# Seven products instead of eight for chunks 8 to 11, with a planner on new costs

## The chip, the cores and the metric

One core of one Trainium2 chip runs the kernel. The metric is the device time of one execution in microseconds. Four runs of the kernel before gave 288.5 to 291.41 us, median 289.25.

## The reference

Two stages follow each other. The first is a linear attention with decay (batch 4, 8 heads, 768 steps, head width 48); the second is a mixture of 4 experts on the 3072 x 384 result.

```python
for t in range(S):                       # attention
    cur = einsum('bhd,bhe->bhde', u * kt, vt)
    y[:, :, t] = einsum('bhd,bhde->bhe', rt, state + cur)
    state = w[None, :, :, None] * state + einsum('bhd,bhe->bhde', kt, vt)
x = y.transpose(0, 2, 1, 3).reshape(B * S, H * D)
p = domain_probs / (domain_probs.sum(-1, keepdims=True) + 1e-09)
for e in range(E):                       # experts; w1 384 x 1024, w2 1024 x 384
    h = maximum(x @ w1[e], 0.0)
    out += p[:, e:e + 1] * (h @ w2[e])
```

## The kernel before, in words

**Tiling.** Time is cut into 24 chunks of 128 steps: chunk `ci` belongs to batch `ci % 4` and is the `ci // 4`-th of it. Four chunks, one per batch, make a group of 512 rows (`sc`, 0 to 5) for the experts.

**Attention of a chunk** (lines 361 to 653). R, K and V are loaded by SyncE (L229). VectorE scales R and K by powers of w ("scale", L394 for chunks from 8 on). GpSimd multiplies R, K and u (L406, L414), VectorE sums over the head ("dcoef", L427), and GpSimd multiplies V by it ("dv", L432). R and K are transposed by TensorE for the first chunks and by a DMA from chunk 8 on (L439). TensorE makes the scores (L506), from chunk 8 on for two chunks in one go; VectorE masks them (L523 for the even chunk, 1024 wide; L520 for the odd one, two halves of 512). TensorE makes Y from the state and the scores (L546, L553), VectorE adds dv (L568), and the state is brought up to date by TensorE (L626), VectorE (L635) and GpSimd (L645).

**Experts.** For groups 0 and 1 (`sc < SCALED`), Y is transposed as it is; the first layer is L700 or L706, its relu is ScalarE's (L715, L717), the second layer is L737, and p enters as its result leaves PSUM (L746, L748). From group 2 on, Y is first multiplied by p of each expert ("Xs", four per chunk, L588 on ScalarE or L590 on VectorE), and a DMA transposes each half (L598, "Xout"), so that the second layer may sum over experts in PSUM. Each half has one buffer (`Yse0`, `Yse1`): the next chunk's Xs waits for the transpose of this one.

**Second layer from group 2 on.** For `sc < FIRST` (only group 2) it is direct: per chunk and expert 8 matmuls of 384 columns (L967, "l2s"), and one ScalarE copy per chunk (L974). For the later groups it is a 2 x 2 block scheme with seven products (`products`, L844 on): the four blocks are two chunks by the even and odd halves of the hidden width, and w2 is cut in the same way and into column halves of 192. VectorE makes sums of hidden blocks ("sum", L873, four per pair of chunks, in halves of the experts for the first pair), and once for all, eight sums of w2's blocks ("mix", L817). TensorE makes the products (L904, 16 matmuls of 192 columns each, in two jobs of 8). Results go through chains in one PSUM bank (`ONTO`), with copies by ScalarE (L925) and adds by VectorE (L927) in between. The last mix overwrites a block of w2, and so waits until all direct second layers are through.

**What sets the order.** Every engine's order is fixed at build time by a list-scheduling planner (L991 on). Each piece of work is a job with a cost per engine, needs, buffers taken and dropped, and a rank, the lower the earlier. The planner keeps a clock per engine, starts the job of lowest rank that is ready and fits, and multiplies costs by `SLOWER` after its own time 85, but for sums, Xs and mixes. `GATES` holds back the scaling of a pair of chunks from 8 on until a named piece of expert work is done. A job with costs for several engines goes to the one that takes it first. On the chip each engine then follows its list in order, and waits only for data and buffers.

**PSUM.** `mm` has four banks, shared by first-layer groups, products and second layers; `tr` one; `ys` one, for Y and state products; `At` two, for the even chunk's scores. The odd chunk's scores take one bank of `tr` and one of `mm`.

Of the kernel before, what the change touches and what calls it, by code (L numbers as in the profile page):

```python
# [19 lines left out]
def kernel(  # L20
# [14 lines left out]
    B, H, S, D = r.shape  # L35
    HD = H * D
    C = 128
# [73 lines left out]
    mask = consts.tile([128, 128], BF16)  # L111
# [10 lines left out]
    for b in range(B):  # L122
# [13 lines left out]

    GATES = [3, 4, 9, 4, 5, 6, 6, 24]
    WARM, NSPIN = 6.6, 6  # L140
    TAIL = {"T": 0.27, "V": 0.17, "A": 0.20, "P": 0.17, "S": 0.0}
    DMAT = 8
# [3 lines left out]
    ATT = ("scale", "ruk_a", "ruk_b", "dcoef", "dv", "T", "Tout", "At", "mask", "Y", "Yout", "X",  # L146
           "Xout", "Sm", "Sv", "S")
    SLOTS = [(0, 0, 1), (1, 0, 0), (0, 1, 1), (1, 1, 1), (2, 0, 0), (2, 1, 0), (3, 0, 0), (3, 1, 0)]
    FIRST = 3
    SCALED = 2  # L150
    ONTO = {6: 1, 5: 6, 3: 5, 4: 7}
    MIX_RANK = 18.0
    XS_ON = {'A': 0.61, 'V': 0.51}
    MIX_ON = {'V': 1.4}
    SCALE_US = 1.2
    VB_ON = {'A': 0.42, 'P': 0.5}
    XS_RANK = 0
    SUM_RANK = -60
    NSH = 4
    SEQ_S = (((1, 0), (3, 0), (2, 0), (1, 1), (3, 1), (2, 1), (4, 0), (4, 1)),  # L160
             ((1, 2), (3, 2), (2, 2), (4, 2)))
    LATE, SLOWER = 85.0, {"V": 1.13, "P": 1.06, "A": 1.15}
    SLOTS += [(e, sc, 0) for sc in range(2, SCALED) for e in range(E)]
    ORDER_P = (1, 2, 6, 7, 4, 5, 3)
    SEQ_P = ((0, 1, 0), (0, 2, 0), (0, 7, 0), (0, 1, 1), (0, 2, 1), (0, 7, 1), (0, 6, 0), (0, 6, 1), (0, 4, 0),
# [5 lines left out]
                 mm=4, xTe=3, hTs=3, oacc=6, Yse0=1, Yse1=1, Tn=2)  # L171
# [7 lines left out]
    def job(name, on, run, needs=(), rank=0.0, takes=(), drops=(), moves=None,  # L179
            behind=()):  # L180
        j = Job()
        j.behind = behind
        j.name, j.on, j.run, j.needs, j.rank = name, on, run, list(needs), rank
        j.takes, j.drops, j.moves = takes, drops, moves
        for k in drops:
            tokens[k] = tokens.get(k, 0) + 1
        j.pad = 0.0
        ci = name[1] if isinstance(name, tuple) and name[0] in ATT else -1
        if ci >= SUB:

            j.pad = PAD_PE if "T" in on else PAD
        j.no = len(jobs)
        assert name not in jobs
        jobs[name] = j
# [37 lines left out]
    at_of = {}  # L232
# [128 lines left out]
    def attention(ci):  # L361
# [4 lines left out]
        rk = float(ci)  # L366
# [25 lines left out]
        us = 0.48 if ci < SUB else 0.65  # L392
# [96 lines left out]


        paired = ci >= DMAT
        tags = ("tr", "mm") if paired and ci % 2 else ("At", "At")

        def at():

            for x in (ci - 1, ci) if paired else (ci,):
                for j in range(2):
                    if paired and x == ci:
                        tag = ("tr", "mm")[j]
                        tl["At", x, j] = psum.tile([128, NP, C], F32, tag=tag, bufs=slots[tag], name="At_ps")  # L500
                    else:
                        at_free.remove(j)
                        tl["At", x, j] = At_all[:, j]
                for q in range(NP):
                    for j in range(2):
                        nc.tensor.matmul(tl["At", x, j][:, q, :],  # L506
                                         tl["RKT", x][j * P2:(j + 1) * P2, 1, q, :],
                                         tl["RKT", x][j * P2:(j + 1) * P2, 0, q, :],
                                         start=True, stop=True)

        split = not paired or ci % 2
# [15 lines left out]
        last = ci + 1 if paired and ci % 2 == 0 else ci  # L527
        if paired and ci % 2:
            job(("At", ci), {"T": 0.64}, at, [("T", ci - 1, 1), ready], on_pe,
                (("At", ci - 1, 0), ("At", ci - 1, 1), ("tr", ci, 0), ("mm", ci, 1)),  # L530
                (("RKT", ci - 1), ("RKT", ci)))
        elif not paired:
            job(("At", ci), {"T": 0.42}, at, [ready] + ([("Tout", ci, 0)] if ci < SUB else []), on_pe,
                (("At", ci, 0), ("At", ci, 1)), (("RKT", ci),))
        for j in range(2 if split else 1):
            job(("mask", ci, j), {"V": 0.61 if split else 1.18}, mk(j), [("At", last)],
                rk - 0.5, (("AtM", ci),) if j == 0 else (), ((tags[j], ci, j),) if split else (("At", ci, 0), ("At", ci, 1)),
                behind=(("mask", ci, 0),) if j else ())

# [34 lines left out]
        sc = ci // SUB  # L574
# [28 lines left out]
        else:  # L603
            tag = "mm" if ci < SUB else "tr"
# [45 lines left out]
        if c == 0:  # L650
            job(("S", ci), {"V": 0.56}, sv, [("Sm", ci), ("Yout", SUB - 1)], rk + 2, (), (("ys", "S", ci),))
        else:
            job(("Sv", ci), {"V": 0.56}, sv, [("Sm", ci)], rk - 0.1, (("Tn", ci),), (("ys", "S", ci),))
            job(("S", ci), {"P": 1.1}, sp, [("Sv", ci)], rk - 0.5, (), (("Tn", ci),))

    y_sb = weights.tile([128, 3 * HD], BF16)
    y_free, y_at = [0, 1, 2], {}
# [186 lines left out]
    def products(sc, q, at0):  # L844
# [12 lines left out]
        at_of = {m: of[m, 0] for m in ORDER_P}  # L857
        no = s_no[0] % (NSH // 2) * 2
        s_no[0] += 1
        s_tok = [(f"S{no + hf}", sc, q) for hf in range(2)]  # L860
# [5 lines left out]
        def sum_job(k, hf):  # L866
            hs = (0, 1) if hf == 2 else (hf,)

            def run():
                o, x, y, op = {1: (None, A21, A22, ALU.subtract), 3: (A21, A21, A11, ALU.subtract),  # L870
                               2: (A11, None, A11, ALU.subtract), 4: (A12, A12, A11, ALU.add)}[k]
                o, x, y = (s1_of(hf) if z is None else a_of(z, hf) for z in (o, x, y))
                nc.vector.tensor_tensor(o, x, y, op=op)  # L873
            needs = all_cast + [n for h in hs for n in relus[h]]
            if k == 3 and q:
                needs.append(("C", sc, 0, 5))
            if k in (2, 4):
                needs += [("P", sc, q, 1 if k == 2 else 2, h) for h in hs]
            job(("sum", sc, q, k, hf), {"V": 1.26 if hf == 2 else 0.74}, run, needs,
                at_of[{1: 6, 3: 6, 2: 6, 4: 3}[k]] + SUM_RANK, tuple(s_tok[h] for h in hs) if k == 1 else (),  # L880
                tuple(x for h in hs for x in hts[h]) + (tuple(s_tok[h] for h in hs) if k in (1, 2) else ()),
                behind=(s_last[0],) if s_last[0] else ())
            s_last[0] = ("sum", sc, q, k, hf)
            for h in hs:
                sum_at[k, h] = s_last[0]
# [30 lines left out]
        for m in ORDER_P:  # L916
            at = at_of[m]

            def c_job(m, s, h, first, drop=()):
                def run():  # L920
                    oacc(c1)
                    o = tl["oacc", c1 // 2][:, s, h * DH:(h + 1) * DH]
                    ps = tl["P", sc, q, m]
                    if first:
                        nc.scalar.copy(o, ps)  # L925
                    else:
                        nc.vector.tensor_add(o, o, ps)  # L927
                needs = [("P", sc, q, m, 1)] + ([] if first else [("C", sc, q, {2: 1, 5: 7, 4: 6}[m])])
                job(("C", sc, q, m), {"A": 0.35} if first else {"V": 0.36}, run, needs, at - 90,
                    (("oacc", c1 // 2),) if m == 1 else (), tuple(("mm", "P", sc, q, x) for x in drop))  # L930
            if m == 1:
                c_job(1, 0, 0, True)
            elif m == 2:
                c_job(2, 0, 0, False, (2,))
                if c2 == TOTC - 1:
                    store(c1, [("C", sc, q, 2)], 0, DH)
            elif m == 6:
                c_job(6, 1, 0, True)
            elif m == 7:
                c_job(7, 1, 1, True)  # L940
            elif m == 5:
                c_job(5, 1, 1, False)
            elif m == 4:
                c_job(4, 1, 0, False, (7,))
                store(c2, [("C", sc, q, 4), ("C", sc, q, 5)])
            else:
                c_job(3, 0, 1, True, (1,))
                if c2 == TOTC - 1:
                    store(c1, [("C", sc, q, 3)], DH, Dm)
                else:  # L950
                    store(c1, [("C", sc, q, 3), ("C", sc, q, 2)])
# [26 lines left out]
    for sc in range(SCALED, NSC):  # L978
        at = 8 * (sc - SCALED) + len(SLOTS)
# [19 lines left out]
    avail = {"T": 3.7, "V": 4.5, "A": 3.3, "P": 1.5, "S": 0.6}  # L999
# [41 lines left out]
    now, seq, n_done = 0.0, 1, 0  # L1041
# [7 lines left out]
    def start(e):  # L1049
# [3 lines left out]
        while waiting[e]:  # L1053
            it = heapq.heappop(waiting[e])
            j = it[2]
# [10 lines left out]
        if got is not None and now < HURRY:  # L1066

            us = got.on[e]
# [8 lines left out]
        j = got  # L1077
# [3 lines left out]
                held.add(t)  # L1081
                free[t[0]] -= 1
        us = j.on[e] * (2.0 if e == "T" and now < WARM and j.name not in ("wmm", "umm") else 1.0)
        if e in SLOWER and now > LATE and j.name[0] not in ("sum", "Xs", "mix"):
            us *= SLOWER[e]
        if j.moves:
            taken, end = dma(now, us, *j.moves)
            us = taken - now + 0.04
# [90 lines left out]
```

## Time and profile before

| | |
|---|---|
| profiled execution | 289.8 us, span 287.8 us |
| TensorE busy | 279.9 us |
| VectorE busy | 181.3 us |
| ScalarE busy | 168.2 us |
| GpSimd busy | 105.5 us |
| first-layer matmuls L706 (512 columns) | 484 records, 113.7 us busy |
| direct second layer of group 2, L967 | 128, 21.9 us busy |
| seven products, L904 (three groups) | 672, 62.7 us busy |
| Xs on VectorE, L590 | 36, 21.1 us busy |
| Xs on ScalarE, L588 | 28, 16.7 us busy |
| operand sums, L873 | 36, 31.4 us busy |
| weight mixes, L817 | 8, 7.5 us busy |

Busy time of a group is counted from the records: neighbours of one engine overlap a little, so sums of busy time run above the stretch that the group fills. Weight loads have a row of their own (PEld) and overlap the matmuls (PE). The chain of waits goes back from the last instruction to what released it each time, and lists the pieces in order of time. "DVE a <- DMA b: total, times, longest" in the list of waits means that VectorE sat idle before a until b's transfer was there. Times in the stretches and the timeline count from the start of the span.

### The profile page before, as it was taken

What the parts mean: (1) busy time and instruction counts of PE and PEld (TensorE: products, weight loads), DVE (VectorE), ACT (ScalarE), POOL (GpSimd) and SP (SyncE); (2) the same over time, 40 slices, a digit from 0 to 9 for tenths busy, and PEclk for the clock granted to TensorE, in tenths of its full rate; (3) what the DMA queues carried; (4) which work ended last, traced back from release to release, by engine and by line L of the source; (5) the groups of instructions that cost most, each with busy time, mean ns of one, the idle gap of its engine ahead of it and who ended that gap; (6) DMA issues with size and microseconds to landing.
All of it is one profiled execution on the core that took longest, in us unless ns stands there. A gap on an engine that the chain in (4) does not pass through costs nothing.

```text
span 287.8 us, 6434 instructions
## 1 busy us (share of the span) xinstructions
PE 279.9 (97%) x2558; PEld 187.6 (65%) x2578; DVE 181.3 (63%) x305; ACT 168.2 (58%) x300; POOL 105.5 (37%) x127
## 2 busy tenths in 40 slices
PE   8898999999999999999999999999999999999995
PEld 3776655866775556444666554699745799544995
DVE  4976967667859978858544897788417473010760
ACT  4672968576848444788641489714588611799210
POOL 2884244462996745046563469801000000000000
PEclk9999999999999999999999999999999999999999
DMA  7998999999999576998859995902530401100011
GB/s 151 238 292 248 320 287 256 217 275 248 232 168 223 110 176 145 214 214 113 162 90 211 210 194 104 154 6 83 139 73 17 95 2 56 57 0 0 2 70 41
DMA packets 130145, 42.41 MB, mean 147 GB/s; under 512 B 118186, under 2 KB 130092, under 8 KB 130116
## 3 DMA queue, kind: packets, MB, share of 16 engines
q1 hardware_dynamic: 130100, 42.01, 66.1%
q8 instruction: 20, 0.33, 0.5%
q14 instruction: 9, 0.07, 0.1%
q10 hardware_dynamic: 16, 0.00, 0.0%
HBM read 26.79 MB, written 4.72 MB: 110 GB/s over the span
## 4 chain that ended last, share of the span: by engine, by line
PE 87%; SPq 6%; DMA 3%; DVE 2%; issue 1%; POOL 0%; ACT 0%; DVEq 0%; ACTq 0%
PE hT_ps L706 36%; PE M_ps L904 19%; PE out_ps L737 14%; PE out_ps L967 7%; PE hT_ps L700 4%; SPq L229 4%; DMA stg<-in_moe_w_dram 3%; PE At_all L506 1%; PE Y_ps L553 1%; PE St_ps L626 1%; SPq L246 1%; PE Y_ps L546 1%; SPq L243 1%; DVE stg L590 1%; PE RKT_ps L458 1%
## 5 line engine op out<-in xcount | busy, mean ns | idle before, releaser
L717 ACT ACTIVATE hAll<-hT_ps 128x512 bf16<-128x512 f32 x168 | 98.6, 597 | 24.8 <-PE hT_ps L706 19.3
L706 PE MATMUL hT_ps<-stg,w_sb 128*128 128x512 bf16 x372 | 85.3, 379 | 0.7
L706 PEld LDWEIGHTS <-w_sb 128*128 128x128 bf16 x504 | 47.4, 98 | 52.2
L904 PEld LDWEIGHTS <-hAll 128*128 128x128 bf16 x576 | 47.6, 98 | 0.8
L737 PE MATMUL out_ps<-w_sb,hAll 128*128 128x384 bf16 x256 | 45.7, 326 | 1.0 <-POOL w_sb L82 1.0
L406 POOL TENSOR_TENSOR ruk<-RKin 128x384 f32<-128x384 f32 x24 | 26.2, 1094 | 46.5 <-DMA RKin<-in_k_dram 27.6
L737 PEld LDWEIGHTS <-hAll 128*128 128x128 bf16 x256 | 24.1, 98 | 16.0 <-issue 1.1
L925 ACT COPY o_sb<-M_ps 128x192 f32<-128x192 f32 x24 | 7.6, 318 | 42.1 <-PE M_ps L904 42.1
L432 POOL TENSOR_TENSOR dv<-Vt,dcoef 128x384 f32<-128x384 f32 x24 | 20.6, 861 | 25.5 <-ACT stg L588 19.7
L706 PE MATMUL hT_ps<-xTe,w_sb 128*128 128x512 bf16 x112 | 28.4, 379 | 0.4
L645 POOL TENSOR_TENSOR S<-Tn,wC 64x192 bf16<-64x192 f32 x32 | 23.2, 725 | 9.5 <-DVE Tn L635 8.3
L904 PE MATMUL M_ps<-w_sb,hAll 128*128 128x192 bf16 x288 | 26.5, 246 | 0.0
L590 DVE TENSOR_SCALAR stg<-dv,p_nat 128x384 bf16<-128x384 f32 x36 | 21.1, 616 | 6.4 <-DMA stg<-stg 6.2
L414 POOL TENSOR_TENSOR ruk<-ruk,U_sd 128x384 f32<-128x384 f32 x23 | 24.3, 1061 | 1.0
L748 DVE SCALAR_TENSOR_TENSOR o_sb<-out_ps,p_nat,o_sb 128x384 f32<-128x384 f32 x24 | 14.6, 614 | 11.7 <-PE out_ps L737 11.7
L967 PE MATMUL out_ps<-w_sb,hAll 128*128 128x384 bf16 x128 | 21.9, 326 | 0.0
L588 ACT ACTIVATE stg<-dv,p_nat 128x384 bf16<-128x384 f32 x28 | 16.7, 610 | 6.9 <-DMA stg<-stg 6.0
L700 PE MATMUL hT_ps<-xTe,w_sb 128*128 128x128 bf16 x288 | 18.0, 219 | 0.2
L715 ACT ACTIVATE hAll<-hT_ps 128x512 bf16<-128x512 f32 x24 | 14.2, 597 | 6.0 <-PE hT_ps L700 5.1
L700 PEld LDWEIGHTS <-w_sb 128*128 128x128 bf16 x288 | 16.7, 98 | 1.1 <-ACT w_sb L78 0.3
L967 PEld LDWEIGHTS <-hAll 128*128 128x128 bf16 x128 | 12.1, 98 | 7.7
L394 DVE TENSOR_TENSOR RK_sb<-RKin,W_both 128x768 bf16<-128x768 f32 x16 | 16.7, 1061 | 0.1
(90 smaller groups left out, 324.6 us busy)
## 6 DMA issues: line engine op xcount, KB each, us to landing
stg<-in_moe_w_dram SPq DMA_DIRECT2D x16, 576.0 KB, 5.9
RKin<-in_k_dram SPq DMA_DIRECT2D x24, 192.0 KB, 3.8
Vt<-in_v_dram SPq DMA_DIRECT2D x24, 192.0 KB, 3.9
RKin<-in_r_dram SPq DMA_DIRECT2D x24, 192.0 KB, 4.2
out_dram<-o_sb SPq DMA_DIRECT2D x23, 192.0 KB, 2.0
stg<-in_moe_w_dram SPq DMA_DIRECT2D x8, 384.0 KB, 6.1
stg<-stg SPq DMA_TRANSPOSE x32, 2.8
RKT<-RK_sb SPq DMA_TRANSPOSE x16, 3.3
```

Of the source, the lines that this page charges most:

```text
L394: job(("scale", ci, 0), {"V": SCALE_US}, lambda: nc.vector.tensor_mul(RK[:, :, :, 0:D], tl["in", ci], W_both), [("Rt", ci), ("Kt", ci), (" ...
L406: nc.gpsimd.tensor_mul(tl["ruk", ci], tl["Rt", ci], tl["Kt", ci])
L414: nc.gpsimd.tensor_mul(tl["ruk", ci], tl["ruk", ci], U_sd)
L432: nc.gpsimd.tensor_mul(tl["dv", ci], tl["Vt", ci], tl["dcoef", ci].to_broadcast((128, H, D)))
L590: nc.vector.tensor_scalar(o, tl["Ysb", ci], scalar1=p_nat[:, e, n_p:n_p + 1], scalar2=None, op0=ALU.mult)
L645: nc.gpsimd.tensor_mul(S_new[pr, :, cl], Tn2[pr, tn_at[ci], :, cl], wC[pr, :, None].to_broadcast((P2, NP, D)))
L700: nc.tensor.matmul(ps[:, i, :], w1_sb[:, e, db, (fb + i) * 128:(fb + i + 1) * 128], xTe[:, db, s0, :], start=(i == 0 and db == 0), stop=(i ...
L706: nc.tensor.matmul(ps[:, 0:n, :].rearrange("p a b -> p (a b)"), w1_sb[:, e, db, fb * 128:(fb + 1) * 128], xTe[:, x0 + db, s0:s0 + n, :].re ...
L717: nc.scalar.activation(hTs[:, fb, s0:s0 + n, :], ps[:, 0:n, :], AF.Relu)
L737: nc.tensor.matmul(ps, relu_tile(e, sc)[:, fb, s, :], w2_sb[:, e, fb, :], start=(fb == 0), stop=(fb == NFB - 1))
L904: nc.tensor.matmul(tl["P", sc, q, m], st, moving(m, hf, n), start=(hf == 0 and n == 0 and m not in ONTO), stop=(hf == 1 and n == 7), skip_ ...
L967: nc.tensor.matmul(tl["o", ci], relu_tile(e, sc)[:, fb, s, :], w2_sb[:, e, fb, :], start=(e == 0 and fb == 0), stop=(e == E - 1 and fb == ...
```

## The change

It moves group 2 (chunks 8 to 11) from the direct second layer to seven products (`FIRST` 3 to 2), so that no direct one of the later kind is left, puts all Xs on ScalarE, changes costs in the planner, lengthens there VectorE's sums, scalings, mixes and Xs by up to 0.6 of what GpSimd is still busy, exchanges the two banks of the odd chunk's scores, and gives the first two operand sums of each group a rank of 0.0 above their place instead of -60, so that they no longer go ahead of masks.

```diff
-    GATES = [3, 4, 9, 4, 5, 6, 6, 24]
+    GATES = [3, 5, 8, 8, 16, 17, 7, 23]
...
-    FIRST = 3
+    FIRST = 2
...
-    MIX_RANK = 18.0
-    XS_ON = {'A': 0.61, 'V': 0.51}
-    MIX_ON = {'V': 1.4}
-    SCALE_US = 1.2
+    MIX_RANK = 16.0
+    XS_ON = {'A': 0.61}
+    MIX_ON = {'V': 0.97}
+    SCALE_US = 0.97
...
+    EARLY_SUM = 0.0
...
+    SHARED = 0.6
...
-        tags = ("tr", "mm") if paired and ci % 2 else ("At", "At")
+        tags = ("mm", "tr") if paired and ci % 2 else ("At", "At")
...
-                        tag = ("tr", "mm")[j]
+                        tag = ("mm", "tr")[j]
...
-                (("At", ci - 1, 0), ("At", ci - 1, 1), ("tr", ci, 0), ("mm", ci, 1)),
+                (("At", ci - 1, 0), ("At", ci - 1, 1), ("mm", ci, 0), ("tr", ci, 1)),
...
-            job(("mask", ci, j), {"V": 0.61 if split else 1.18}, mk(j), [("At", last)],
+            job(("mask", ci, j), {"V": 0.61 if split else 1.09}, mk(j), [("At", last)],
...
-            job(("Sv", ci), {"V": 0.56}, sv, [("Sm", ci)], rk - 0.1, (("Tn", ci),), (("ys", "S", ci),))
-            job(("S", ci), {"P": 1.1}, sp, [("Sv", ci)], rk - 0.5, (), (("Tn", ci),))
+            job(("Sv", ci), {"V": 0.5}, sv, [("Sm", ci)], rk - 0.1, (("Tn", ci),), (("ys", "S", ci),))
+            job(("S", ci), {"P": 1.3}, sp, [("Sv", ci)], rk - 0.5, (), (("Tn", ci),))
...
-            job(("sum", sc, q, k, hf), {"V": 1.26 if hf == 2 else 0.74}, run, needs,
-                at_of[{1: 6, 3: 6, 2: 6, 4: 3}[k]] + SUM_RANK, tuple(s_tok[h] for h in hs) if k == 1 else (),
+            job(("sum", sc, q, k, hf), {"V": 1.23 if hf == 2 else 0.7}, run, needs,
+                at_of[{1: 6, 3: 6, 2: 6, 4: 3}[k]] + (EARLY_SUM if k in (1, 3) and not q and not hf else SUM_RANK), tuple(s_tok[h] for h in hs) if k == 1 else (),
...
-                job(("C", sc, q, m), {"A": 0.35} if first else {"V": 0.36}, run, needs, at - 90,
+                job(("C", sc, q, m), {"A": 0.3} if first else {"V": 0.33}, run, needs, at - 90,
...
-        if e in SLOWER and now > LATE and j.name[0] not in ("sum", "Xs", "mix"):
+        if e in SLOWER and now > LATE and j.name[0] not in ("sum", "Xs", "mix", "scale"):
             us *= SLOWER[e]
+        if e == "V" and now > LATE and j.name[0] in ("sum", "scale", "mix", "Xs"):
+            us += SHARED * min(us, max(0.0, avail["P"] - now))
```

## Prediction

> **What bounds the kernel now.** I read the page first, then the chain that ended last, then the busy time in stretches of 8 us, then the waits.
>
> From the page, engine totals and two of the forty-slice rows:
>
> ```profile
> PE 279.9 (97%) x2558; PEld 187.6 (65%) x2578; DVE 181.3 (63%) x305; ACT 168.2 (58%) x300; POOL 105.5 (37%) x127
> ...
> PE   8898999999999999999999999999999999999995
> ...
> PEclk9999999999999999999999999999999999999999
> ```
>
> TensorE is busy 279.9 of 287.8 us, in nine tenths or more of every slice after the first ones, at its full clock. Busy is not proof of peak, so I check the pace: in the chain, the 512-wide first-layer products stand as 12 in 2.59 us, 0.216 us each, and no other engine but TensorE sits on the chain for more than a few us after 32 us. A stall put in is therefore paid in full, and TensorE work taken out is gained in full, as long as nothing new is late.
>
> From the chain, in order of time (start, length, what, count): the direct second layer of chunks 8 to 11 (L967), and two blocks of seven-product work (L904), of chunks 16 to 19 and 20 to 23:
>
> ```profile
> 138.71 1.30 PE out_ps L967 x8
> ...
> 140.38 2.60 PE out_ps L967 x16
> ...
> 143.15 2.60 PE out_ps L967 x16
> ...
> 145.92 2.60 PE out_ps L967 x16
> ...
> 148.69 2.60 PE out_ps L967 x16
> ...
> 151.46 6.50 PE out_ps L967 x40
> ...
> 158.52 2.71 PE out_ps L967 x16
> ...
> 226.99 18.48 PE M_ps L904 x224
> ...
> 266.19 18.49 PE M_ps L904 x224
> ```
>
> The same work for four chunks is 128 instructions in 1.30+2.60x4+6.50+2.71 = 20.91 us one way, and 224 in 18.48 the other.
>
> **The change part by part.**
>
> *FIRST 3 to 2: chunks 8 to 11 get seven products.* It removes 16 jobs of 8 matmuls (128 x 384 columns, 20.91 us) and 4 ScalarE copies, and adds 28 jobs of 8 (224 x 192 columns), 12 VectorE sums, 6 VectorE adds and 8 ScalarE copies. On TensorE: 18.48 - 20.91 = **-2.4 us**. A rule speaks against it. The Trainium skill, "TensorE: Matmul & The Clock Gate", section LDWEIGHTS, gives a weight load as columns/1.2 ns: 107 ns for 128 columns, and its section on the back-to-back issue gap says that load and product together set the spacing. If each of 224 products took its load's 107 ns, they would cost 23.9 us, and the change would lose 3.0. The rows decide: the loads do show 98 ns each, but 8 us of the seven-product stretch hold 100 products:
>
> ```profile
> 232.00:240.00 8.00, 8.00 (x100) 8.00 (x98) 5.04 (x7) 0.96 (x3) 0.00 (x0) 1.00 0.14 52
> ```
>
> That is (columns: stretch, its length, then busy of PE, PEld, DVE, ACT, POOL) 80 to 82.5 ns per product with PEld also full, so loads overlap each other; 18.48 is measured twice and I take it.
>
> *The eight weight mixes (L817) and sums need VectorE earlier.* The mixes were spread over 116 to 162 us, two of them held until L967 was through; now all eight, four 768-wide scalings, the masks and two sums stand before the first product. Tally for the first layer of chunks 8 to 11 up to the last mask that TensorE needs there: 1 eviction 0.61, 8 mixes x 0.95, 4 scalings x 0.95, 2 wide masks x 1.22, 4 narrow x 0.68, 2 half sums x 0.69, 2 dcoef x 0.54, 2 Y adds x 0.55 = 20.0, less about 0.08 for each of 24 neighbours that overlap (two mixes stand as 1.81) = 18. TensorE in the same stretch: 32 groups x 0.648, two pairs of score products x 0.55, three Y x 0.37 = 22.9. About 5 us of room, part of which goes into waiting for inputs. The layout of the queues leaves the closest Y job some 1 us behind its mask. Cost: 0; without the cover, about 1 us.
>
> *VectorE beside GpSimd.* The Trainium skill, "GPSIMD Engine Reference", section Specifications, says that GpSimd shares VectorE's SBUF interfaces and contends with instructions that have two SBUF inputs, and sums, mixes and scalings are such. The trace has both prices for a half sum, GpSimd busy and idle:
>
> ```profile
> 175.57 0.88 DVE L873 TENSOR_TENSOR hAll<-hAll 128x1024 bf16<-128x1024 bf16 x1
> ...
> 187.18 0.69 DVE L873 TENSOR_TENSOR hAll<-hAll 128x1024 bf16<-128x1024 bf16 x1
> ```
>
> The new sums are 16 halves' worth, so 0 to 3.2 us more of VectorE. GpSimd is busy 60% where they now stand, so some 1.9:
>
> ```profile
> 136.00:144.00 8.00, 8.00 (x70) 4.85 (x69) 4.37 (x9) 5.09 (x10) 3.83 (x5) 1.00 0.80 154
> 144.00:152.00 8.00, 8.00 (x60) 5.03 (x59) 3.75 (x6) 4.01 (x8) 4.98 (x7) 1.00 0.62 105
> ```
>
> VectorE under the new products: 16 x 0.61 + 1.9 + 6 adds x 0.28 + 4 state adds x 0.5 + two small ones 1.0 = 16.4, against 18.48 + 4 x 0.17 = 19.2 on TensorE. Covered, though in order: the closest pair is a product that reuses a bank behind a ScalarE copy (two products, 1.32 us, between; copy 0.32, two hand-overs of 0.1 as from Y to its add), room 0.8. The same order already runs for chunks 12 to 23 without a gap, but now with scalings (Xs) mixed in on ScalarE. Cost 0 to 1 us.
>
> *XS_ON: all 64 scalings by p on ScalarE.* 36 leave VectorE:
>
> ```profile
> L590 DVE TENSOR_SCALAR stg<-dv,p_nat 128x384 bf16<-128x384 f32 x36 | 21.1, 616 | 6.4 <-DMA stg<-stg 6.2
> ...
> L588 ACT ACTIVATE stg<-dv,p_nat 128x384 bf16<-128x384 f32 x28 | 16.7, 610 | 6.9 <-DMA stg<-stg 6.0
> ```
>
> VectorE -21.1 us; ScalarE +36 x 0.5 (back to back they stand 0.50 apart) = +18, and with 8 copies for 4 about +19, to 187 of 285: not the bound. But ScalarE works in order, and behind a scaling that waits for a transpose (its two half buffers are single) stand relus that free TensorE's banks. The first layer turns over 4 banks: three further groups, 1.94 us, less the relu 0.60 and hand-overs 0.2, so a relu may be 1.1 us late for nothing. The waits moved were these:
>
> ```profile
> DVE stg L590 <- DMA stg<-stg: 6.2, 9, 1.7
> ...
> ACT stg L588 <- DMA stg<-stg: 6.0, 6, 2.5
> ```
>
> Fifteen, 12.2 us in all, 0.8 on average, below 1.1. Most fall to second layers and products, where no relu is queued. Cost: 0 to 3 us, by the mean wait nearer 0. SyncE is in order too: a transpose that waits for its scaling holds the loads and stores behind it. The R, K, V loads are four chunks ahead, so I give that nothing.
>
> *Bank tags mm/tr exchanged* for odd chunks' scores: the shared mm bank goes back after the first narrow mask rather than the second, 0.6 us earlier, eight times; no row shows anyone waiting for it: 0. *Planner numbers, SHARED, GATES*: no instruction by themselves, only the order. TensorE keeps the same groups, scores, Y and state products; SyncE keeps 32 + 16 transposes, 25 stores and all loads, in another order. The first 50 us are unchanged in order. EARLY_SUM puts two sums between masks: 2 x 0.69 ahead of a Y add that no one awaits within 2 us: 0.
>
> **Sum.** -2.4 on TensorE; stalls 0 to about 5 by the upper ends (1 + 1 + 3), taken as 0.3. Span 287.8 - 2.1 = 285.7; that execution took 289.8, 2.0 more than its span, so 287.7 beside 289.8. The median of the runs shown is 289.25, 0.55 less, which gives **287.1**.
>
> **The rivals.**
> - *Given back* : the closest places (Y behind masks, product behind copy) are each late by about half a microsecond, in four blocks: 4 x 0.5 = 2.0, 288.9. For it: VectorE's 18 of 22.9 and 16.4 of 19.2 leave little in a fixed order. Against: 21.1 us left that engine.
> - *ScalarE holds the relus* (slower): if the 15 waits, all in its queue now, average 1.5 us instead of 0.8, each stalls the first layer by 0.4: 15 x 0.4 = 6.0, 286.85 + 6.0 = 292.9. It costs more than the gain from an average of 1.26, and over 1% from 1.45. For it: the longest was 2.5, on this engine. Against: the mean, and where they stand.
> - *No gain on TensorE*: the weight loads set the pace after all (98 ns): 224 x 0.098 = 21.95, +1.0, 290.3. Against: two blocks at 82.5 ns.
> - *More than the sum*: no gap is left to close after 32 us, so only scatter (288.5 to 291.41 before) or the 0.2 us hand-overs would bring it under 286.4.
>
> **How the numbers follow.** Likeliest, gain kept: 0.64, own range 286.2 to 288.2. Given back: 0.21 at 288.9. ScalarE: 0.09 at 292.9. No gain: 0.02. More than the sum, 0.04, at 286.2. A measurement of this kernel can tell about 1% (2.9 us) from no change. Faster by over 1%, below 286.4: the last case and the lower edge of the likeliest, 0.14. Slower by over 1%, above 292.1: ScalarE's case and a tail of the second, 0.10. Else 0.76. Range 286.0 to 290.0: the first two cases nearly whole.
>
> **What would show it.** Right: no L967; 896 products at L904 near 82.5 ns, each block of 224 in 18.5 to 19.5 us; TensorE's first layers still 12 in 2.59 us; L588 x64 with waits for transposes of 8 to 14 us in all; L873 x48. Wrong: idle of TensorE before L706 released by ScalarE (relus late), before L904 released by VectorE or ScalarE (sums or copies late), before L553 by VectorE (masks late), or a span that ends after 287.

## The result, and the profile after

The kernel after takes 287.19 us at the median of 43 runs, the kernel before 288.97 at the median of 64 in the same comparisons: ratio 0.9938, 95% interval 0.9925 to 0.9951, 1.8 us less. A second set gave 0.9940 (0.9917 to 0.9964). The profiled execution took 286.4 us, its span 284.5.

The page of the kernel after, engine totals, TensorE's slices and its clock, then the scalings:

```profile
PE 277.1 (97%) x2654; PEld 193.2 (68%) x2674; DVE 178.5 (63%) x287; ACT 185.5 (65%) x339; POOL 107.3 (38%) x128
...
PE   7999999999999999999999999999999999999995
...
PEclk9999999999999999999999999999999999999999
...
L590 ACT ACTIVATE stg<-dv,p_nat 128x384 bf16<-128x384 f32 x64 | 36.7, 608 | 4.7 <-DMA stg<-stg 4.7
```

TensorE is still the bound, busy 277.1 us with 96 more matmuls (224 of 192 columns in place of 128 of 384). VectorE is down by 3 us on balance, ScalarE up by 17.

The chain of the kernel after, where the direct second layer stood before, and the last two groups:

```profile
137.73 0.68 PE M_ps L906 x8
138.43 0.69 DVE hAll L875
139.12 1.25 DVE stg L875
140.39 0.70 DVE hAll L875
141.14 4.79 PE M_ps L906 x56
...
146.10 4.62 PE M_ps L906 x56
...
150.89 1.98 PE M_ps L906 x24
...
223.74 18.48 PE M_ps L906 x224
...
262.94 18.49 PE M_ps L906 x224
```

No L967 (it would be L969) is left. The last two blocks still take 18.5 us each. In the new block, three sums of VectorE stand on the chain before TensorE goes on at 141.14: a first, small loss.

**Reading three parts instead of one span.** The profiled spans differ by 3.3 us, the medians by 1.8. I cut each trace at two places: where the first 512-wide first-layer product starts, and where the first layer of chunks 8 to 11 starts. In TensorE's timelines these are, in the kernel before and in the kernel after:

```profile
31.07 0.81 PE L706 MATMUL hT_ps<-xTe,w_sb 128*128 128x512 bf16 x2
...
115.40 5.99 PE L706 MATMUL hT_ps<-stg,w_sb 128*128 128x512 bf16 x26
```

```profile
29.25 0.81 PE L708 MATMUL hT_ps<-xTe,w_sb 128*128 128x512 bf16 x2
...
114.04 8.16 PE L708 MATMUL hT_ps<-stg,w_sb 128*128 128x512 bf16 x36
```

The lengths, in us ("start" up to the first cut, "middle" between them, "rest" from the second to the end):

| kernel | start | middle | rest | span |
|---|---|---|---|---|
| before | 31.07 | 84.33 | 172.40 | 287.8 |
| after | 29.25 | 84.79 | 170.46 | 284.5 |
| after, second set | 30.46 | 84.67 | 170.17 | 285.3 |

The start changes from execution to execution (29.2 to 31.6 us over all traces here); in the kernel before, TensorE there waits 1.0 us for the cast of a weight. The middle is the same to 0.5 us. What the change does lies in the rest: -1.9 and -2.2 us. The experiments are read by this table and by their times.

### The profile page after: what moved, and what is told of

Read it like the earlier page. It is cut to its first block, busy times and chain, and to the rows that moved or that the text cites. A ratio compares the mean times of both kernels' runs of the same rounds, so it can differ in the third digit from the quotient of the medians.

```text
span 284.5 us, 6646 instructions
## 1 busy us (share of the span) xinstructions
PE 277.1 (97%) x2654; PEld 193.2 (68%) x2674; DVE 178.5 (63%) x287; ACT 185.5 (65%) x339; POOL 107.3 (38%) x128
## 4 chain that ended last, share of the span: by engine, by line
PE 85%; DMA 7%; SPq 4%; DVE 2%; ACT 1%; issue 1%; ACTq 0%
PE hT_ps L708 36%; PE M_ps L906 23%; PE out_ps L739 14%; PE hT_ps L702 5%; DMA stg<-in_moe_w_dram 3%; SPq L231 3%; DMA Vt<-in_v_dram 2%; PE Y_ps L555 2%; DMA stg<-stg 1%; PE At_all L508 1%; PE Y_ps L548 1%; SPq L245 1%; PE St_ps L628 1%; PE At_ps L508 1%; PE RKT_ps L460 1%
## 5 line engine op out<-in xcount | busy, mean ns | idle before, releaser
L719 ACT ACTIVATE hAll<-hT_ps 128x512 bf16<-128x512 f32 x168 | 98.7, 597 | 20.4 <-PE hT_ps L708 13.8
L708 PEld LDWEIGHTS <-w_sb 128*128 128x128 bf16 x504 | 47.2, 98 | 52.3 <-DMA stg<-stg 0.2
L739 PE MATMUL out_ps<-w_sb,hAll 128*128 128x384 bf16 x256 | 45.7, 326 | 0.3 <-DVE w_sb L80 0.3
L590 ACT ACTIVATE stg<-dv,p_nat 128x384 bf16<-128x384 f32 x64 | 36.7, 608 | 4.7 <-DMA stg<-stg 4.7
L750 DVE SCALAR_TENSOR_TENSOR o_sb<-out_ps,p_nat,o_sb 128x384 f32<-128x384 f32 x24 | 14.6, 616 | 15.6 <-PE out_ps L739 15.4
L875 DVE TENSOR_TENSOR hAll<-stg,hAll 128x1024 bf16<-128x1024 bf16 (+1 forms) x12 | 11.2, 933 | 20.0 <-PE M_ps L906 19.4
L875 DVE TENSOR_TENSOR hAll<-hAll 128x1024 bf16<-128x1024 bf16 (+1 forms) x24 | 22.5, 953 | 0.2
L875 DVE TENSOR_TENSOR stg<-hAll 128x1024 bf16<-128x1024 bf16 (+1 forms) x12 | 11.4, 948 | 11.9 <-ACT hAll L719 11.9
L906 PE MATMUL M_ps<-w_mix,hAll 128*128 128x192 bf16 x192 | 18.6, 246 | 0.0
L525 DVE TENSOR_TENSOR AtM<-At_all,mask 128x1024 bf16<-128x1024 f32 x8 | 9.8, 1220 | 13.4 <-PE At_all L508 13.4
L906 PE MATMUL M_ps<-o_sb,hAll 128*128 128x192 bf16 x192 | 18.0, 246 | 0.1
```

What stands on the lines that cost most here:

```text
L590: nc.scalar.mul(o, tl["Ysb", ci], p_nat[:, e, n_p:n_p + 1])
L708: nc.tensor.matmul(ps[:, 0:n, :].rearrange("p a b -> p (a b)"), w1_sb[:, e, db, fb * 128:(fb + 1) * 128], xTe[:, x0 + db, s0:s0 + n, :].re ...
L719: nc.scalar.activation(hTs[:, fb, s0:s0 + n, :], ps[:, 0:n, :], AF.Relu)
L739: nc.tensor.matmul(ps, relu_tile(e, sc)[:, fb, s, :], w2_sb[:, e, fb, :], start=(fb == 0), stop=(fb == NFB - 1))
L750: nc.vector.scalar_tensor_tensor(oacc(ci), in0=tl["o", e, ci], scalar=pe, in1=oacc(ci), op0=ALU.mult, op1=ALU.add)
L906: nc.tensor.matmul(tl["P", sc, q, m], st, moving(m, hf, n), start=(hf == 0 and n == 0 and m not in ONTO), stop=(hf == 1 and n == 7), skip_ ...
```

## The experiments

My theory: seven products give TensorE 2.4 us less, and the new order keeps them fed, less about 0.5 us. Rivals: the gain is the new order's, not the products'; the products gain nothing because weight loads pace them; ScalarE has no room. Ratios are to the kernel before on the same chip.

**Direct second layer again, all else new.**

```diff
-    FIRST = 2
+    FIRST = 3
```

> The kernel after, with FIRST back at 3: chunks 8 to 11 have the direct second layer again, everything else of the change stays. If the gain is TensorE's work alone (20.9 us direct against 18.5 in seven products), this stands at the time of the kernel before, 289.0 (ratio 0.998 to 1.002). If the new order, the new costs and the scalings on ScalarE bring part of the gain by themselves, it is below 0.997, 288.1 or less. If the new order costs something that the seven products pay for, it is above 1.002.

Measured: 288.54 us, ratio 0.9975 (0.9951 to 0.9999). Start 29.73, middle 84.47, rest 172.10. In the trace the rest is 0.3 us below the kernel before, and 1.6 above the kernel after: there the products make most of the difference, and the new order by itself little. The ratio, just under the band expected for "products alone", gives the order 0.7 us, but its interval runs from 0 to 1.4, so the times alone do not divide the gain.

**Seven products alone, all else old.**

```diff
-    FIRST = 3
+    FIRST = 2
```

> The kernel before, with FIRST at 2 and nothing else: seven products for chunks 8 to 11 under the old costs, gates and scalings on both engines. If the old order can carry it, it gains nearly as much as the whole change: 287.0 to 287.5 (ratio 0.993 to 0.995). If the new costs and gates are needed to keep VectorE's mixes, masks and sums in time, part or all is given back: 288 to 291 (ratio 0.997 to 1.007), with idle of TensorE before L904 or L553 in the stretch from 115 to 160 us.

Measured: 292.59 us, ratio 1.0125 (1.0098 to 1.0152), beyond even the second expectation. From TensorE's list of waits in this kernel, those that lie in the rest:

```profile
PE St_ps L626 <- DVE dv L568: 1.0, 1, 1.0
PE St_ps L626 <- DVE Tn L635: 1.0, 1, 1.0
PE M_ps L904 <- DVE w_sb L817: 0.5, 1, 0.5
PE M_ps L904 <- DVE o_sb L927: 0.5, 1, 0.5
```

VectorE's queue at that place, in its timeline:

```profile
143.36 1.85 DVE L873 TENSOR_TENSOR stg<-hAll 128x2048 bf16<-128x2048 bf16 x1
145.13 0.55 DVE L568 TENSOR_TENSOR dv<-Y_ps,dv 128x384 f32<-128x384 f32 x1
145.60 0.94 DVE L817 TENSOR_TENSOR w_mix<-w_sb,w_mix 128x1536 bf16<-128x1536 bf16 x1
146.47 0.54 DVE L635 TENSOR_TENSOR Tn<-S,St_ps 128x384 f32<-128x384 bf16 x1
146.93 0.94 DVE L817 TENSOR_TENSOR w_sb<-w_sb 128x1536 bf16<-128x1536 bf16 x1
147.80 0.54 DVE L635 TENSOR_TENSOR Tn<-S,St_ps 128x384 f32<-128x384 bf16 x1
148.27 0.94 DVE L817 TENSOR_TENSOR w_sb<-w_sb 128x1536 bf16<-128x1536 bf16 x1
```

VectorE works here without a gap until 149.2, and TensorE follows it step by step. Y and the state products share one bank, so a first state product waits for the Y add, which stands behind a sum of 1.85 us, and a second one for a state add, which stands behind a mix. Then products wait for the last two mixes themselves. The rest is 175.73 us, 5.3 over the kernel after. The listed waits are 3.0 us of that, and a stretch in which TensorE's clock was halved is about 1.5 more (last section). So the planner's part is needed, and as cover, not as a gain.

**Seven products and scalings on ScalarE, but old costs, gates, ranks and tags.** The edit before, and:

```diff
-    XS_ON = {'A': 0.61, 'V': 0.51}
+    XS_ON = {'A': 0.61}
```

> The kernel before with seven products for chunks 8 to 11 and all scalings on ScalarE, but the old costs, gates, ranks and bank tags. Seven products alone gave 292.6 us: TensorE starved at 144 to 152 us for weight mixes that stood late in VectorE's queue. If the scalings on VectorE were what made the mixes late, they now come in time and this is within 0.3% of the kernel after, 287 to 288. If the mixes' own rank and cost (1.4 us in the planner, 0.87 on the chip) put them late, TensorE starves there again: 290 or more. Both: between.

Measured: 290.44 us, ratio 1.0021 (1.0001 to 1.0040); rest 172.61. Between, as "both" would have it: taking the scalings from VectorE recovers 3.1 of the 5.3 us in the rest (about half of that because the clock did not fall in this trace), the new costs, gates, ranks and tags the other 2.1. TensorE waits here 1.2 us for sums and 0.4 for a mix.

**The whole change, scalings on both engines.**

```diff
-    XS_ON = {'A': 0.61}
+    XS_ON = {'A': 0.61, 'V': 0.51}
```

> The kernel after, with the scalings by p allowed on VectorE again, as before. If their move to ScalarE is neutral (ScalarE and VectorE both have room), within 0.2% of the kernel after: 286.7 to 287.7, ratio to before 0.992 to 0.996. If VectorE needed the relief, its sums and masks come late: 288 or more (ratio over 0.997). If ScalarE's queue is what costs the small stalls seen in the products of chunks 16 to 19 (0.26 us), it is a little faster: 286.6 to 286.9.

Measured: 288.84 us, ratio 0.9999 (0.9978 to 1.0020): the whole gain is gone. Rest 172.57. The way is another than I had expected; TensorE waits for transposes:

```profile
PE hT_ps L708 <- DMA stg<-stg: 2.1, 2, 1.7
```

These two waits make up the difference to the kernel after in the rest. The longer one is for the scaled Y of chunk 19, the last that the next first layer needs. Its course, in the rows of VectorE, ScalarE, SyncE and TensorE:

```profile
198.99 0.56 DVE L570 TENSOR_TENSOR dv<-Y_ps,dv 128x384 f32<-128x384 f32 x1
...
201.31 0.63 DVE L592 TENSOR_SCALAR stg<-dv,p_nat 128x384 bf16<-128x384 f32 x1
```

```profile
199.63 1.63 ACT L590 ACTIVATE stg<-dv,p_nat 128x384 bf16<-128x384 f32 x3 [1.35 <-DVE dv L570]
```

```profile
201.43 0.34 SPq L786 DMA_DIRECT2D out_dram<-o_sb  x1
201.85 1.21 SPq L600 DMA_TRANSPOSE stg<-stg  x1
```

```profile
204.72 1.46 PE L708 MATMUL hT_ps<-stg,w_sb 128*128 128x512 bf16 x5 [1.75 <-DMA stg<-stg]
```

The scalings start as soon as the Y add is done. It is this Y add that is late: 5.7 us ahead of the first layer that needs it, where the kernel after has 20.8 (180.31 to 201.09). TensorE runs without a wait from 159.2 to the products of that Y, so it is the planner that has put them there. The transpose that TensorE waits for, issued at 201.85, needs scalings of ScalarE alone, the last of which ended at 201.26; VectorE's ended only at 201.94 and belongs to the other half. It stood in SyncE's queue behind an output store that waited 1.4 us for an add of VectorE, and landed 2.7 us after its issue. At the group before, the Y add of the last chunk is late too (5.9 us ahead instead of 12.6), and the wait is 0.33 us. So what costs the gain is the order that the planner makes with two engines for the scalings, not a scaling that came late on VectorE. `GATES` and the ranks were left as they are for one engine; whether others would save the gain with both is not shown. Sums and masks were in time.

**Products in two halves of 96 columns.**

```diff
-                for n in range(8):
-                    st = s1_of(hf)[:, n, :] if m == 5 else ...
-                    nc.tensor.matmul(tl["P", sc, q, m], st, moving(m, hf, n), ...
+                for z in range(2):
+                    for n in range(8):
+                        st = s1_of(hf)[:, n, :] if m == 5 else ...
+                        nc.tensor.matmul(tl["P", sc, q, m][:, z * 96:(z + 1) * 96], st,
+                                         moving(m, hf, n)[:, z * 96:(z + 1) * 96], ...
```

> The kernel after, with each product of 192 columns made as two of 96 over the same weights: twice the weight loads, the same columns, the same result. If the columns streamed set the pace down to there (40 ns each), the block of 224 stays near 18.5 us and the time near 287 to 290. If a weight load sets the pace, each of 448 in a block takes what a load takes: at the 82 ns now seen, 36.7 us a block, +73 us for four (360 us); at 107 ns, the rule's figure, +118 us (405 us). In between: half a load's shown 98 ns, 49 ns each, 22 us a block, +14 us (301 us).

Measured: 288.94 us, ratio 1.0002 (0.9981 to 1.0024). The chain of this kernel, the last two blocks:

```profile
224.98 19.04 PE M_ps L907 x448
...
264.74 19.05 PE M_ps L907 x448
```

448 products of 96 columns, each with a load of its own, take 19.04 us: 42.5 ns each, and 0.56 us a block more than 224 of 192. Four blocks make 2.2 us; the rest grew by 2.2. In 8 us this kernel shows the load row full and the product row full with twice the count:

```profile
232.00:240.00 8.00, 8.00 (x193) 8.00 (x191) 4.38 (x6) 2.02 (x6) 0.00 (x0) 1.00 0.60 102
```

So a load of 128 columns costs at most 42.5 ns of spacing, and the columns set the pace: 42.5 ns at 96, 82.5 at 192. With the 216 of the 512-wide products these lie on one line, 0.417 ns a column and 2.5 ns a product, in which no part of a load is to be seen. That rival falls. A load's shown length, 98 ns, is not what it costs; a full row of loads says nothing about a bound here.

**Every scaling on ScalarE twice.**

```diff
                         nc.scalar.mul(o, tl["Ysb", ci], p_nat[:, e, n_p:n_p + 1])
+                        nc.scalar.mul(o, tl["Ysb", ci], p_nat[:, e, n_p:n_p + 1])
```

> The kernel after, with each of the 64 scalings on ScalarE done twice in a row, the order of the rest unchanged (some 32 us more of ScalarE). If ScalarE has the room that the prediction gave it, in the products, and 1.1 us of cover for a relu in the first layers, little is lost: 288 to 290. If a scaling in front of a relu or of a copy out of PSUM is paid by TensorE, about half of the 32 us shows: 300 and more. Estimate: the first layers of chunks 16 to 23 are at 89% on ScalarE and get 3 to 4 us more each, and the copies in the products come late by 0.5 us some eight times: 292 to 296.

Measured: 299.51 us, ratio 1.0337 (1.0309 to 1.0365), some 12 us over the kernel after for 32 us of work, above my estimate. TensorE's waits in it:

```profile
PE M_ps L907 <- ACT o_sb L928: 6.1, 6, 1.9
PE hT_ps L709 <- ACT hAll L720: 1.1, 3, 0.5
```

About half goes into copies out of PSUM that stand behind scalings, six times, 1.9 us at most; relus cost 1.1. The cover for relus holds well, that for copies does not: with one product bank chained to the next, a copy has the 1.3 us of two products. ScalarE has room in total and little in the products.

**First operand sums ahead of masks again.**

```diff
-    EARLY_SUM = 0.0
+    EARLY_SUM = -60
```

> The kernel after, with the first two operand sums of each group at their old rank, ahead of the masks. If their place costs nothing (there is room of 1 us and more behind each mask), the time is that of the kernel after, ratio to before 0.992 to 0.996. If two half sums of 0.69 us ahead of a mask make the Y jobs late, about 0.5 us in each of four groups: 289, ratio 0.999 or more.

Measured: 287.81 us, ratio 0.9931 (0.9909 to 0.9953); rest 170.78. No difference that these runs can tell.

**No lengthening of VectorE beside GpSimd in the planner.**

```diff
-    SHARED = 0.6
+    SHARED = 0.0
```

> The kernel after, with VectorE not lengthened beside GpSimd in the planner (SHARED 0). Few jobs change their place. If that lengthening matters, sums or masks stand too tight and TensorE waits 1 us or more: ratio to before 0.997 or more. If it only shifts a few jobs within their room, ratio 0.992 to 0.996.

Measured: 287.58 us, ratio 0.9945 (0.9922 to 0.9967); rest 170.48. No difference.

**Bank tags as before.**

```diff
-        tags = ("mm", "tr") if paired and ci % 2 else ("At", "At")
+        tags = ("tr", "mm") if paired and ci % 2 else ("At", "At")
```

(and the same exchange where the bank is allotted and taken)

> The kernel after, with the two banks of the odd chunks' scores as before (tr first, mm second), nothing else. Priced at nothing in the prediction, as no row shows a wait for the bank: ratio to before 0.992 to 0.996. If the bank that comes free 0.6 us earlier is what lets the first layer run through beside the masks, TensorE waits about 0.5 us in each of up to eight places: ratio 0.998 or more.

Measured: 287.11 us, ratio 0.9932 (0.9905 to 0.9959); rest 170.09. No difference.

**Transfers landing later in the planner, from its time 24 on.**

```diff
-    MARGIN, SLACK = 1.06, 0.0
+    MARGIN, SLACK = 1.06, 1.0
```

> The kernel after, with 1.0 us more of landing time for every transfer in the planner, so that scalings that wait for a transpose stand behind the copies out of PSUM rather than ahead of them. If the two small stalls in the products (0.27 us behind a sum beside GpSimd, 0.26 behind a copy that stood behind a waiting scaling) are what separates the kernel after from its sum, and this order cures the second and costs nothing elsewhere, 286.9 (ratio to before 0.992 to 0.994). If the changed order moves waits elsewhere, 287.5 or more.

Measured: 291.72 us, ratio 1.0058 (1.0026 to 1.0090). The rest is 169.98 us, the shortest of all, but the middle 87.84, 3.1 longer than in the kernel after: TensorE is idle for 2.6 us ahead of the first layer of chunks 8 to 11. SyncE's timeline there, and then TensorE's chain:

```profile
114.86 1.52 SPq L786 DMA_DIRECT2D out_dram<-o_sb  x3
116.48 1.25 SPq L600 DMA_TRANSPOSE stg<-stg  x1
```

```profile
119.32 2.75 PE hT_ps L708 x12
```

The scalings of the first half of chunk 11 ended at 114.25. Their transpose was issued 2.2 us later, behind three output stores, the last of which waited for VectorE until 116.03. Such transposes take 2.8 us from issue to landing at the median, which leads to 119.3, when TensorE starts. This is read from the trace; no run exchanged the stores and the transpose. The median holds a second loss: four of the eight executions ran at a lower mean clock (last section).

**The same, only from the planner's time 112 on.**

```diff
-        return taken, b + us + DMA_END + (SLACK if now > 24 else 0.0)
+        return taken, b + us + DMA_END + (1.0 if now > 112 else 0.0)
```

> The kernel after, with 1.0 us more of landing time for transfers in the planner only from its own time 112 on. The earlier run with it from 24 us on lost 3.4 us ahead of chunks 8 to 11 and ran the rest in 170.0 us, 0.5 less than the kernel after. If the place of the scalings behind the copies is what cures the small stalls, this keeps the early part as in the kernel after and ends 0.3 to 0.5 us before it: ratio to before 0.991 to 0.993. If the cure came from the other early order, it is like the kernel after or a little slower.

Measured: 287.31 us, ratio 0.9943 (0.9924 to 0.9961); middle 84.33, rest 170.29. The early loss is gone, but a gain over the kernel after (0.9938 and 0.9940) is not to be seen. No kernel here is faster than the kernel after by more than the runs can tell.

**The kernel after, second set.**

> The kernel after once more, unchanged, beside the three others on the same chip: ratio to before 0.992 to 0.996, as measured first. In the trace, the start up to the first 512-wide product varies with when the weights land (29.3 to 31.6 us in the traces so far); from the first layer of chunks 8 to 11 to the end 170.5 us again.

Measured: 287.17 us, ratio 0.9940; rest 170.17.

## Why the prediction was right, point by point

*287.1 against 287.19, within the range.* That the two agree to 0.1 us is luck: the prediction took 2.1 us from a median of 289.25, and the many runs show 1.8 less than 288.97. The pieces:

- **TensorE, -2.4 us: right.** The blocks took 18.48 and 18.49 us again, the new one 19.44 less four state products of 0.17, 18.76, of which 0.27 is the first stall below. Direct against seven in the otherwise same kernel: 1.6 us in the rest, 1.9 against the second set.
- **The weight-load rule: the prediction was right to go by the row** of 100 products in 8 us, and the split into 96 shows by how far: a load costs 42.5 ns at most, not 98 or the rule's 107.
- **Stalls, 0.3 taken: 0.53 found**, both in products. The first is the three sums on the chain above. One of them ran beside GpSimd's product for chunk 15. VectorE's timeline, then GpSimd's:

```profile
138.43 0.69 DVE L875 TENSOR_TENSOR hAll<-stg,hAll 128x1024 bf16<-128x1024 bf16 x1 [1.96 <-PE M_ps L906]
139.04 1.32 DVE L875 TENSOR_TENSOR stg<-hAll 128x1024 bf16<-128x1024 bf16 x1
140.39 0.69 DVE L875 TENSOR_TENSOR hAll<-hAll 128x1024 bf16<-128x1024 bf16 x1
```

```profile
138.57 1.24 POOL L434 TENSOR_TENSOR dv<-Vt,dcoef 128x384 f32<-128x384 f32 x1 [4.69 <-ACT stg L590]
```

  The half sum took 1.32 us instead of 0.69 between two that took 0.69, and TensorE went on at 141.14, 0.27 late. The prediction had 0.88 for a half sum beside GpSimd; this one cost nearly twice its idle price. The second stall is a copy behind two scalings (of chunk 18) that waited for a transpose, in the products of chunks 12 to 15:

```profile
182.22 4.19 DMA stg<-stg
...
186.52 1.12 ACT stg L590 x2
187.64 0.21 ACT o_sb L927
...
187.90 1.48 PE M_ps L906 x16
```

  The products before it end at 187.64, so 0.26 lost. The prediction named both kinds of place; of the first it gave the cover as product behind copy, where it was product behind sum. -2.43 + 0.53 = -1.90 against -1.94 in the rest. The trace of the second set has only the first stall, and its rest is 0.29 shorter.
- **VectorE ahead of the products: 18 of 22.9 was too low.** The items listed add up to 20.7, not 20.0, so 18.8 with the overlaps taken off. The stretches of that first layer and of the new products in the kernel after (length, then busy time of PE, PEld, DVE, ACT and POOL):

```profile
114.04:137.57 23.53, 23.37 (x175) 11.74 (x177) 21.05 (x27) 19.67 (x35) 6.33 (x6) 1.00 0.79 163
137.57:157.01 19.44, 19.33 (x247) 19.11 (x243) 15.58 (x23) 11.10 (x25) 11.53 (x14) 1.00 0.62 123
```

  In the first layer VectorE was busy 21.05 us of 23.53. The two half sums ran beside GpSimd and took 1.07 and 1.48 us instead of 0.69 each (+1.2), and one reduction and one Y add more than listed fell into the stretch (+1.1). The Y jobs came through without a wait, but the 5 us of room were 2.5. Seven products alone show what it costs when it fails. Under the new products the forecast held: 15.6 us busy of 19.4, for 16.4 of 19.2.
- **ScalarE: the size was wrong, the sign right.** I expected waits for transposes of 8 to 14 us in its queue; there were 4.7 in five, 1.4 at the longest; probably since one engine that does all four scalings of a chunk reaches the next chunk's later, which I did not test. The rival needed an average of 1.5; it was 0.9. But "ScalarE is not the bound" held only in total: doubled scalings cost some 12 us for 32.
- **XS_ON was undervalued.** I counted it as VectorE's relief, and expected of its undoing late masks and sums. Undone, it takes the whole gain (0.9999), by an order in which the last Y of a group comes late, and so the transposes that feed the next first layer, a place that the prediction did not name.
- **SyncE at nothing: right for the kernel after,** where no first layer waits for a transpose. The prediction looked only at transfers that stand behind a transpose. In two experiments a transpose stood behind output stores, ahead of waits of 1.75 and 2.6 us.
- **Tags, SHARED, EARLY_SUM at nothing: right** as far as these runs can tell (their intervals reach 0.2 to 0.3% to either side).

## What to carry to other kernels

On a kernel whose tensor engine never waits, price a change by the tensor engine's own spacing in the chain, and then look for the first queue in which a needed job stands behind others: the same 2.4 us were worth -1.8, 0 or +3.6 us by where a few dozen small jobs stood. Cut the trace at two or three fixed events and compare the parts; the span alone mixed 1.8 us at the start, which changes from execution to execution, with 1.9 us of effect. When work may move between engines, a planner makes another order for everything: look at what it moved elsewhere, and follow the work to the transfer that it feeds and to what stands ahead of that transfer in its queue, not only to the engine that it leaves.

## What the runs showed of the hardware that I had not expected

When TensorE starved in seven products alone, its clock fell. Its stretches there, with the columns of before: length, busy of PE, PEld, DVE, ACT and POOL, then the granted clock:

```profile
146.00:147.00 1.00, 0.08 (x2) 0.00 (x0) 1.00 (x3) 0.88 (x2) 0.00 (x0) 1.00 0.00 0
147.00:148.00 1.00, 0.40 (x5) 0.25 (x5) 1.00 (x3) 1.00 (x3) 0.91 (x1) 1.00 0.00 0
148.00:149.00 1.00, 1.00 (x12) 1.00 (x13) 1.00 (x2) 1.00 (x3) 0.93 (x2) 0.79 0.10 21
149.00:150.00 1.00, 0.89 (x7) 0.71 (x6) 0.60 (x2) 0.58 (x2) 0.92 (x2) 0.50 0.90 175
150.00:151.00 1.00, 1.00 (x11) 0.94 (x10) 1.00 (x2) 0.00 (x0) 1.00 (x2) 0.50 0.84 165
151.00:152.00 1.00, 1.00 (x9) 0.92 (x7) 0.30 (x1) 0.51 (x1) 0.93 (x2) 0.51 0.17 32
152.00:153.00 1.00, 0.88 (x11) 0.73 (x10) 0.68 (x3) 0.09 (x1) 0.87 (x3) 1.00 0.41 77
```

After some 3 us at a quarter busy, from 144.7 to 147.9, the clock was 0.50 from about 148.6 to 152.0, when TensorE was busy again: a job of eight products took 1.21 to 1.44 us there instead of 0.66. So waits of 3 us, the longest single one 1.03, brought a second loss of about 1.5 us (an estimate: half speed over 3.4 us, part of it waiting anyway).

In the profiled executions, single gaps of 1.75 us (scalings on both engines) and 2.6 us (transfers landing later from time 24 on) left the clock at 1.00. The mean clock of each execution says more. A stretch like the one above makes the mean clock of an execution 0.994. Of seven products alone, five of six executions had 0.993 or 0.994; of transfers landing later from time 24 on, four of eight, and these took 291.95 to 292.91 us, the others 289.79 to 291.49. Of the kernel before, 6 of 104 had 0.994 (291.0 to 292.3 us, where the median is 289), of the kernel after none of 51. So the gap of 2.6 us probably costs the clock in about half of the executions. Where the clock fell in executions that were not profiled, nothing here shows.
